# Transposed scores on array tiles and a second softmax built on VectorE, in a fused cross-attention and maxout kernel

## The chip, the cores and the metric

The kernel runs on one core of one Trainium2 chip. The metric is the device time of the whole kernel in microseconds (us), of which several executions are taken. A core has a matrix engine (TensorE, PE in the profile; PEld are its weight loads), VectorE (DVE), ScalarE (ACT), GpSimd (POOL) and SyncE (SP), which here only issues transfers. Each engine works through its own instructions in order and waits for the others by semaphores. Matrix products land in a memory called PSUM, of which the kernels use eight banks; VectorE or ScalarE empties a bank ("evacuates" it) before TensorE uses it again.

## The reference

Per batch b and head h (8 each), x is 512 tokens by 64 and the state is 32 rows (n) by 64. There are two attentions over the same scores, one normalized over the 32 rows, one over the 512 tokens; then a feed-forward layer with a maximum over three products.

```python
scores  = scale * x @ state.T;   a  = softmax(scores,  over n)        # 512 x 32
xread   = a @ state
scores2 = scale * state @ x.T;   a2 = softmax(scores2, over tokens)   # 32 x 512
sread   = a2 @ x
y = concatenate([xread, sread], over tokens), heads side by side      # 8 x 544 rows, 512 wide
h = maximum(y @ w1, y @ w2, y @ w3)                                   # 768 wide
out = h @ w_out
```

The kernels work in bf16 with f32 sums. Both fold the state into the weights: M = state @ w (the "M units") is made per batch, and the product y @ w of the token rows becomes a @ M, so xread is never formed.

## The kernel before

Everything is ordered by hand: a list of short words says what is issued when. `idle n` stands for n filler matmuls on zeros, `lx`, `lw`, `lo` for loads, `pm` for the permutation and cast of x, `xT` for its transposes on TensorE and `xb` for those by a transposing transfer (the "crossbar"), `S` for scores and softmax, `aT` and `ab` for the transposes of a, `R` for the state reads (sread), `M` for M units, `u` for one product a @ M with its evacuation, `o` for half an output tile. In the profile these are known by their PSUM tiles: px (transposes of x), ps (scores), pr (state reads), pa (transposes of a), pm (M units), pw (products a @ M), po (output products), pz (fillers).

```python
OPENING = """
id, idle 9, sel, idle 9, pm 0 0 a, pm 0 1 v, lx 1, xT 0 0 v, lw 2 4, pm 1 1 v, pm 1 0 v,
xT 0 1 a, idle 8, lw 1 2, lw 0 1, S 0 0 g, S 0 1 g, xT 1 1 a, xT 1 0 a, R 0, lw 4 6,
... (cut)
PERIOD = """
u u u P L S S o o u M M m o u u o u u u o u u o X u M m m R u o u u u o u u
"""
# ... cut
def scores(b, h, eng):
    ps = bank([128, 2, 2, HP, Ns], F32, "ps")
    for jj in range(2):
        for hp in range(HP):
            mm(ps[:, jj, :, hp, :], xT(b)[:, 2 * h + jj, hp, :], sbd[:, b, hp, :, :], ...)
    # ... exp on ScalarE to e; reduce over n, reciprocal, product a = e * rden
def state_reads(b):
    # ... cut: pd = ones.T @ e gives the sums over tokens, 8 matmuls in 128x64 mode
    for hp in range(HP):
        for j in range(J):
            mm(psr[:, hp, :, :], x_nat(b)[:, j, 2 * hp:2 * hp + 2, :], e[:, j, :, hp, :], ...)
    # ... cut: AT = psr * reciprocal(pd)
def up(g, m, i):
    pw = bank([128, S], F32, "pw")
    for par in range(2):
        mm(pw, M_sb[:, g, m, par, i, :], aT(g)[:, :, par, :], par == 0, par == 1)
    # i = 0: ScalarE copies pw to t;  i = 1, 2: VectorE takes the maximum of t and pw
```

Tokens lie on the partitions: a softmax over n is then a reduction along the free axis, but a needs a transpose before it can multiply M.

The softmax here doesn't subtract the row's maximum and nothing guards it: scores larger than these inputs give would overflow.

## Time and profile before

| | before |
|---|---|
| time, median (range) | 159.68 us (159.11 to 159.83, 4 runs) |
| span of the profiled run | 157.9 us |
| busy PE / DVE / ACT / POOL | 150.1 / 111.9 / 94.7 / 44.4 us |
| first product pw starts | 18.01 us |
| start of reads in the middle | every 15.66 us |
| last matmul ends (modelled) | 154.4 us, 3.5 us ahead of the end |

TensorE is at 95%, and the chain that ended last is TensorE's for the most part. (This chain is the work followed back from the last instruction, at each step to what released it.) The page's chain part gives the shares of the span by engine:

```profile
PE 79%; DMA 10%; POOL 4%; ACT 3%; issue 1%; DVE 1%; SPq 0%; POOLq 0%
```

What is not TensorE's in it lies in the first 31 us and in the tail.

### The profile page before, as it was taken

The numbers are of one execution on the slowest core, as the hardware profiler recorded it, in microseconds if no ns is written. First come the engines' busy times: TensorE is split into PE (matmuls) and PEld (weight loads), VectorE is DVE, ScalarE is ACT, GpSimd is POOL, SyncE is SP. The second block draws the span as 40 slices with busy tenths as digits, with TensorE's granted clock in tenths as the row PEclk, the third lists the DMA queues.
The fourth block names the chain that finished last, engine by engine and source line by source line (L and its number), as shares of the span: only waits on it lengthen the run. The fifth ranks groups of instructions, "written<-read, shape, count | busy, mean of one in ns | idle before, by whom it ended". The sixth has DMA issues, their size and how long they took to land.

```text
span 157.9 us, 3558 instructions
## 1 busy us (share of the span) xinstructions
PE 150.1 (95%) x1387; PEld 75.4 (48%) x1404; DVE 111.9 (71%) x200; ACT 94.7 (60%) x188; POOL 44.4 (28%) x48
## 2 busy tenths in 40 slices
PE   6988999999999999999999999999999999999991
PEld 2456353354455454444444544454444567754450
DVE  3257999787569788968896888688868844378601
ACT  3559978758545855686567656764777433344340
POOL 8926970292530830091008001300130000000000
PEclk9999999999999999999999999999999999999999
DMA  5999999969549499909990609260316033030263
GB/s 153 291 194 188 182 163 179 204 85 188 162 65 252 106 211 125 254 18 170 160 263 25 184 0 243 59 171 0 137 44 156 4 133 133 0 133 4 66 191 141
DMA packets 34400, 21.46 MB, mean 136 GB/s; under 512 B 19536, under 2 KB 31824, under 8 KB 34384
## 3 DMA queue, kind: packets, MB, share of 16 engines
q0 software_dynamic: 14400, 6.82, 33.9%
q1 hardware_dynamic: 19840, 14.29, 33.4%
q8 instruction: 11, 0.18, 0.4%
q10 hardware_dynamic: 144, 0.13, 0.2%
q14 instruction: 5, 0.04, 0.1%
HBM read 15.20 MB, written 8.91 MB: 153 GB/s over the span
## 4 chain that ended last, share of the span: by engine, by line
PE 79%; DMA 10%; POOL 4%; ACT 3%; issue 1%; DVE 1%; SPq 0%; POOLq 0%
PE pw L106 38%; PE po L106 28%; DMA x<-in_x_dram 10%; PE pm L106 4%; PE pr L106 3%; PE ps L106 2%; POOL a L246 2%; PE px L109 1%; ACT M_sb L101 1%; POOL xn L103 1%; PE pz L106 1%; ACT e L238 1%; ACT xn L101 1%; PE pa L109 1%; POOL x L153 1%
## 5 line engine op out<-in xcount | busy, mean ns | idle before, releaser
L106 PE MATMUL pw<-aT,M_sb 128*128 128x512 bf16 x288 | 71.9, 379 | 0.0
L106 PE MATMUL po<-wout,ht 128*128 128x512 bf16 (+1 forms) x194 | 51.1, 373 | 0.8
L304 DVE TENSOR_TENSOR t<-t,pw 128x512 bf16<-128x512 bf16 (+1 forms) x54 | 35.4, 656 | 19.0 <-PE pw L106 8.9
L300 ACT CAST t<-pw 128x512 bf16<-128x512 f32 (+1 forms) x54 | 30.6, 568 | 29.1 <-PE pw L106 28.8
L106 PEld LDWEIGHTS <-M_sb 128*128 128x128 bf16 x288 | 27.0, 98 | 30.8 <-issue 0.8
L306 DVE TENSOR_TENSOR ht<-t,pw 128x512 bf16<-128x512 bf16 (+1 forms) x54 | 35.2, 657 | 6.8 <-PE pw L106 3.0
L246 POOL TENSOR_TENSOR a<-e,rden 128x512 bf16<-128x512 bf16 x16 | 16.4, 1043 | 59.3 <-ACT e L238 36.3
L101 ACT CAST M_sb<-pm 128x384 bf16<-128x384 f32 x75 | 31.0, 505 | 1.3 <-PE pm L106 0.6
L101 ACT COPY o<-po 128x512 f32<-128x512 f32 x32 | 18.8, 586 | 18.6 <-PE po L106 16.1
L106 PEld LDWEIGHTS <-ht 128*128 128x128 bf16 x210 | 19.7, 98 | 21.3 <-issue 1.9
L103 POOL COPY xn<-x 128x2048 bf16<-128x2048 bf16 x6 | 11.3, 1889 | 8.1 <-DMA x<-in_x_dram 8.1
L106 PE MATMUL pm<-W,sbd 64*32 64x384 bf16 x384 | 12.4, 327 | 0.3 <-DMA W<-in_moe_w_dram 0.2
L242 DVE TENSOR_REDUCE den<-e 128x16 f32<-128x512 bf16 x16 | 10.6, 661 | 2.3 <-ACT e L238 2.2
L238 ACT ACTIVATE e<-ps 128x512 bf16<-128x512 f32 x16 | 9.0, 598 | 4.6 <-PE ps L106 4.6
L103 DVE CAST M_sb<-pm 128x384 bf16<-128x384 f32 x21 | 10.6, 534 | 0.0
L144 POOL DMA_DIRECT2D W<-in_moe_w_dram x12 | 9.1, 772 | 3.4 <-DMA x<-in_x_dram 2.9
L106 PE MATMUL pw<-AT,W 128*128 128x256 bf16 x72 | 9.2, 273 | 0.1
L106 PE MATMUL pz<-zeros 128*128 128x512 bf16 x25 | 7.8, 470 | 1.2 <-DVE zeros L125 1.2
L106 PEld LDWEIGHTS <-sbd 64*32 64x32 bf16 x384 | 4.3, 89 | 9.5 <-issue 8.9
L106 PEld LDWEIGHTS <-W 128*128 128x128 bf16 x72 | 7.0, 98 | 2.5
L279 DVE RECIPROCAL rd<-pr 128x128 f32<-128x128 f32 x8 | 7.6, 944 | 0.1
L153 POOL DMA_DIRECT2D x<-in_x_dram x7 | 6.6, 943 | 0.1
(39 smaller groups left out, 66.9 us busy)
## 6 DMA issues: line engine op xcount, KB each, us to landing
out_dram<-o SPq DMA_DIRECT2D x14, 512.0 KB, 2.9
x<-in_x_dram POOLq DMA_DIRECT2D x7, 512.0 KB, 7.9
W<-in_moe_w_dram POOLq DMA_DIRECT2D x6, 256.0 KB, 7.9
x<-in_x_dram SPq DMA_DIRECT2D x1, 1024.0 KB, 6.6
W<-in_moe_w_dram POOLq DMA_DIRECT2D x6, 128.0 KB, 10.9
wout<-in_moe_w_out_dram POOLq DMA_DIRECT2D x1, 768.0 KB, 12.7
out_dram<-o SPq DMA_DIRECT2D x3, 256.0 KB, 2.1
st<-in_state_dram SPq DMA_DIRECT2D x1, 512.0 KB, 3.7
```

The source lines that it names most:

```text
L101: nc.scalar.copy(out=o, in_=i)
L103: ENG[eng].tensor_copy(out=o, in_=i)
L106: nc.tensor.matmul(out_ap, lhsT, rhs, start=start, stop=stop, tile_position=pos)
L144: nc.gpsimd.dma_start(out=W[:, i, :, c], in_=w_v[i][:, :, c])
L153: nc.gpsimd.dma_start(out=x_sb[b].rearrange("p h j d -> p h (j d)"), in_=x[b].rearrange("h (p j) d -> p h (j d)", j=J))
L238: nc.scalar.activation(out=e.rearrange("p r n -> p (r n)"), in_=ps.rearrange("p j a hp n -> p (j a hp n)"), func=AF.Exp, scale=scale)
L242: nc.vector.reduce_sum(out=den, in_=e, axis=AX.X)
L246: ENG[eng].tensor_mul(out=a_of(b)[:, 2 * h:2 * h + 2].rearrange("p j a hp n -> p (j a hp) n"), in0=e, in1=rden.unsqueeze(2).to_broadcast(( ...
L279: nc.vector.reciprocal(out=rd, in_=pd.rearrange("p (hp n) -> p hp n", hp=HP))
L300: nc.scalar.copy(out=t[:, :nn], in_=pw[:, :nn])
L304: nc.vector.tensor_max(t[:, :nn], t0[:, :nn], pw[:, :nn])
L306: nc.vector.tensor_max(ht[:, m, :nn], tiles["t", g, m][:, :nn], pw[:, :nn])
```

## The change

The intent is to take work off TensorE. The scores are made transposed, rows (head, n) on the partitions and 512 tokens along the free axis, by eight matmuls on eight 64x32 tiles of the array. Then a @ M needs no transposes of a. The softmax over tokens becomes a free-axis matter: the exp gives its row sums as a by-product, and a scalar product scales; its result a2 goes through the crossbar back to token rows for the state reads, which lose their eight matmuls for the sums. The softmax over n now crosses partitions; VectorE does it with a reduce that transposes 32x32 blocks and a 32x32 transpose. Some maxima pass through ScalarE (`w` units). The loads of the opening are re-ordered, and a tiny GpSimd copy ("held") keeps the other loads back until the first half of x has landed. All the order lists are new.

```diff
-id, idle 9, sel, idle 9, pm 0 0 a, pm 0 1 v, lx 1, xT 0 0 v, lw 2 4, pm 1 1 v, pm 1 0 v,
-xT 0 1 a, idle 8, lw 1 2, lw 0 1, S 0 0 g, S 0 1 g, xT 1 1 a, xT 1 0 a, R 0, lw 4 6,
 ... (cut)
+id, lx 1, p0 0 0 v, p0 0 1 v, ca 0 v, p0 1 0 a, ca 1 v, xT 0 0 a, p0 1 1 v, lw 0 1, sel,
+lw 2 4, xT 0 1 v, S 0, pm 1 1 g, pm 1 0 v, lw 4 6, idle 11, D 0 0 g, xT 1 0 a, xT 1 1 v,
+D 0 1 v, M 0 0 aa, lx 2, S 1, D 1 0 g, M 1 0 aa, idle 9, u 0 0 0, M 0 3 aa, D 1 1 g,
+lw 1 2, lx 3, M 0 2 av, M 1 2 aa, u 0 0 1, u 0 0 2, u 0 3 0, u 0 3 1, lo, E 0 g,
 ... (cut)
+u 0 1 2, M 1 4 va, xb 3, S 2, u 0 5 2, u 1 1 1 v, E 2 g, u 1 1 2, R 0 a, u 1 4 0,
+o 0 0 0 a, lx 4, u 1 4 1, o 0 0 1 a, M 2 4 av, M 2 5 av, D 2 0 g, R 1 a, eb 2, o 0 1 0 v,
+o 0 1 1 a, M 2 3 aa, M 2 2 aa, M 2 0 aa, u 1 5 2, o 0 2 0 a, o 0 2 1 a, o 0 3 0 a,
+o 0 3 1 a, D 2 1 v, M 2 1 vv, S 3, u 1 4 2, R 2 v
 PERIOD = """
-u u u P L S S o o u M M m o u u o u u u o u u o X u M m m R u o u u u o u u
+e w u w X w w u o P u w o u u u m m M O B L o w u R M M M d w o u u o u S w O o
 ... (cut)
+    def hold():
+
+        if not held:
+            held.append(const.tile([128, 1], F32, name="held"))
+            nc.gpsimd.tensor_copy(out=held[0], in_=x32[:, 0, 0, 0:1])
 ... (cut)
+    def scores(b):
+        ps = [bank([128, S], F32, "ps") for _ in range(2)]
+        for hp in range(HP):
+            for par in range(2):
+                r = slice(par * 64, par * 64 + 64)
+                mm(ps[par][hp * 32:(hp + 1) * 32, :], sT[r, b, hp, :], xT(b)[r, :, hp, :],
+                   True, True, pos=(par * 64, hp * 32))
+        den2 = tile_of("den2", b, att3, [128, 2], F32)
+        for par in range(2):
+            nc.scalar.activation(out=e_of(b)[:, par, :], in_=ps[par], func=AF.Exp, scale=scale,
+                                 accum_out=den2[:, par:par + 1])
+
+    def softmax_n(b, par, eng):
+
+
+        p = slice(0, 2) if par is None else slice(par, par + 1)
+        k = S // 32 * (2 if par is None else 1)
+        e = e_of(b)[:, p, :].rearrange("p a t -> p (a t)")
+        den = att2.tile([128, 2 * S // 32], F32, tag="den", name="den")[:, 0:k]
+        nc.vector.tensor_reduce(out=den, in_=e.rearrange("p (k n) -> p k n", n=32), axis=AX.X,
+                                op=mybir.AluOpType.add, apply_transpose=True)
+        rden = att2.tile([128, 2 * S // 32], BF16, tag="rden", name="rden")[:, 0:k]
         with nc.allow_low_precision("softmax denom reciprocal"):
             nc.vector.reciprocal(out=rden, in_=den)
-        ENG[eng].tensor_mul(
-            out=a_of(b)[:, 2 * h:2 * h + 2].rearrange("p j a hp n -> p (j a hp) n"),
-            in0=e, in1=rden.unsqueeze(2).to_broadcast((128, 16, Ns)))
-
-    def a_crossbar(b):
+        rb = att2.tile([128, 2 * S], BF16, tag="rb", name="rb")[:, 0:32 * k]
+        nc.vector.transpose(out=rb.rearrange("p (k n) -> p k n", n=32),
+                            in_=rden.unsqueeze(2).to_broadcast((128, k, 32)))
+        ENG[eng].tensor_mul(out=aT(b)[:, p, :].rearrange("p a t -> p (a t)"), in0=e, in1=rb)
+
+    def softmax_t(b, eng):
+        rden2 = att2.tile([128, 2], F32, tag="rden2", name="rden2")
+        nc.vector.reciprocal(out=rden2, in_=tiles["den2", b])
 ... (cut: a2T = e * rden2, one scalar product of 128x512 for each parity)
+    def a2_crossbar(b):
         nc.sync.dma_start_transpose(
+            out=a2(b).rearrange("p a j hp n -> p (a j) (hp n)"),
+            in_=a2T(b).rearrange("p a t -> p (a t)"))
 ... (cut)
+    def state_reads(b, eng):
+        pr = bank([128, HP, 2, Ns], F32, "pr")
         for hp in range(HP):
             for j in range(J):
-                mm(psr[:, hp, :, :], x_nat(b)[:, j, 2 * hp:2 * hp + 2, :], e[:, j, :, hp, :],
+                mm(pr[:, hp, :, :], x_nat(b)[:, j, 2 * hp:2 * hp + 2, :], a2(b)[:, :, j, hp, :],
 ... (cut)
+                nc.scalar.copy(out=t[:, :nn], in_=pw[:, :nn])      # "w" units, i == 1
+                tiles["late", g, m] = eng
 ... (cut)
+            if late:
+                ENG[late].tensor_max(h, h, tiles["t", g, m, 1][:, :nn])
```

In the new lists `S` makes the scores, `D` is the softmax over n, `E` the softmax over tokens, `eb` (in a period `X`) the crossbar transfer of a2; `p0` and `ca` permute and cast batch 0's x and the state in pieces, and `B` is the crossbar's transpose of x. In a period, capital and small letters of a pair (`o` and `O`, `E` and `e`) do the same work with different engines.

## The prediction

> **What bounds the kernel now.** I read the page's busy shares first, then the chain that ended last, then the groups, then the timeline of the opening. The page's head:
>
> ```profile
> span 157.9 us, 3558 instructions
> ...
> PE 150.1 (95%) x1387; PEld 75.4 (48%) x1404; DVE 111.9 (71%) x200; ACT 94.7 (60%) x188; POOL 44.4 (28%) x48
> ...
> PE   6988999999999999999999999999999999999991
> ```
>
> TensorE (PE) is full from the fifth of 40 slices to the last but one. Being busy does not prove it the bound, so I looked at the chain in order of time, in the middle of the run (start us, us, what):
>
> ```profile
> 74.04 0.92 PE pr L106 x24
> ...
> 80.14 0.47 PE ps L106 x16
> ...
> 82.33 0.61 PE pm L106 x24
> ...
> 89.70 0.92 PE pr L106 x24
> ```
>
> Nothing but matmuls lies between. State reads (pr) return after 89.70 - 74.04 = 15.66 us, one period (one batch). Matmuls of 512 columns follow each other in 0.216 us there (ten pw take 2.16 us). A period holds 36 pw (7.78 us) and 24 po (5.18), two groups of M units (pm, 0.61 each), the scores ps (0.47) and the reads pr (0.92): 15.57 us. So the middle is TensorE's instruction stream to within 1%, and only fewer or cheaper matmuls can shorten it.
>
> The opening is bound otherwise. From the timeline:
>
> ```profile
> 1.20 4.02 PE L106 MATMUL pz<-zeros 128*128 128x512 bf16 x9 [1.20 <-DVE zeros L125]
> ...
> 7.85 1.04 ACT L101 CAST xn<-x 128x1024 bf16<-128x1024 f32 x1 [0.62 <-DMA x<-in_x_dram]
> ...
> 11.58 0.63 PE L106 MATMUL ps<-sbd,xT 128*128 128x64 bf16 x16
> ...
> 18.01 1.04 PE L106 MATMUL pw<-aT,M_sb 128*128 128x512 bf16 x4
> ```
>
> Batch 0 lands at 7.85, scores start at 11.6, and the first real product (pw) at 18.0; pz is filler. The last matmul ends near 154.45; copy and store of the last half tile take 3.45 more to 157.9. The timed value is 1.8 us over the span (159.67 against 157.9).
>
> Bookkeeping of useful TensorE work: pw 288 x 0.216 = 62.2; pw of the state rows 72 x 0.108 = 7.8; po 204 x 0.216 = 44; 48 M units x 0.2 = 9.8; ps 8 x 0.47 = 3.8; pr 8 x 0.92 = 7.4; px 6 x 0.45 = 2.7; pa 1.9. Sum 139.5. Some 5.5 of it (scores 0 and 1, four px, one pr, pa of batch 0, five M units) lies before 18.0. After 18.0 there are 134.0 of work in 136.4 us, so all holes together are 2.4 us. Most of them lie in the first overlap of batches 0 and 1, not in the periods.
>
> **What the Trainium skill says.** "TensorEngine Tiling (Array Packing)", Tiling Modes: 64x32 gives 8 independent tiles that run in parallel, and a change of mode drains the engine. The trace agrees: in the chain 24 pm take 0.61 us and 16 take 0.45, so eight matmuls of 384 columns cost 0.16 us, the time of one at full clock, plus about 0.13 for the two changes of mode. "TensorE: Matmul & The Clock Gate", Part 1: matmuls run at half clock until about 3.4 us of activity. The trace agrees: nine pz of 512 columns in 4.02 us at the start (0.43 each), 0.216 later. "VectorE: DVE Perf Modes", the perf-mode tier table: reduce runs at one element a cycle, a two-tensor operation on bf16 in SBUF at two, copies and scalar products at four, with about 150 cycles fixed. The trace agrees with two rows: the reduce of 512 took 661 ns, the bf16 copy xn of 1024 took 423 ns ((256+150)/0.96). The other forms are new here, so their times are estimates from that page.
>
> **The change part by part.**
>
> Scores. Sixteen 64-column matmuls against zero-padded weights become eight of 512 columns on eight tiles: 0.16 x 512/384 + 0.13 = 0.34 us instead of 0.47. Saves 0.13 x 8 = 1.0.
>
> State reads. The eight ones-matmuls for the token denominator go, since exp gives the row sums (accum_out). In the timeline they run from 73.97 to the next group's start at 74.32, and a mode change goes with them: about 0.40. Saves 8 x 0.40 = 3.2.
>
> Array transposes of a (batches 0 to 2): pieces of 0.40, 0.40, 0.55, 0.55. Saves 1.9. The xbar transposes (DMA) move from a to a2, off TensorE.
>
> So TensorE work falls by 6.1 to 133.4, and a period from 15.66 to about 15.1. M units, pw, po and px stay.
>
> VectorE, per period. Goes: two reduces (1.32), their reciprocals (0.50), reciprocal rd (0.94), two scaled AT (0.58), three of the six t maxima (3 x 0.687 = 2.06), one M copy (0.51): 5.9. Comes: transposing reduce over 1024, (1024+150)/0.96 = 1.22; reciprocal of 32, 0.35 (between 253 ns for 16 and 944 for 128); 32x32 transpose 1.22; product of 1024 in bf16 0.69; two scalar products 0.29 each; three late maxima SBUF to SBUF (256+150)/0.96 = 0.42 each; two AT copies 0.58; a tiny reciprocal 0.17: 6.1. It stays at about 13.2 us in 15.1, 88%.
>
> ScalarE, per period: three more copies of pw ("w" units with i = 1), 3 x 0.57 = 1.7, and one more M copy, 0.4. From about 10.3 to 12.5 us of 15.1, 83%. GpSimd loses the products a (two of 1.04) and keeps one permutation of 1.9.
>
> So in the periods TensorE stays the bound, but with two evacuating engines both well over 80%, in order, on eight PSUM banks. I allow 0.1 to 0.3 us of holes a period.
>
> The opening. x of batch 0 comes in two halves with the state between, and GpSimd holds all other loads until the first half is in. From the old landing times (state, 0.5 MB, at 4.4; 1.5 MB by 7.85) I put the halves at 4.4 and 8.0. ScalarE has the second half's cast before the copy of xT's first half, so scores 0 come near 10.2 (11.6 before). But x of batch 1 is now issued at 4.4 instead of 1.44; issue to landing was 5.8 to 9.7 us, so it lands at 10.2 to 13. On VectorE its permutation stands ahead of the first softmax: 0.42, then reduce, reciprocal, transpose for the first parity (0.66 + 0.25 + 0.69), a product on GpSimd (1.04), behind its own permutation and three W issues of 0.77. The second parity ends about as late. aT of batch 0 is whole at 15 to 17, and the order has nine fillers (1.9 us) just before the first pw. I put that pw at 16.5, against 18.0.
>
> Before it fewer useful matmuls have run: two score sets (0.7), px 1.8, two M units 0.4, so 133.4 - 2.9 = 130.5 remain. With the old 2.4 us of holes the end is 16.5 + 130.5 + 2.4 + 3.45 = 152.85 in span, 154.6 timed. The overlap of batches 0 and 1 is tighter, though: from first pw to the third state read TensorE has about 27 us, and my counts give ScalarE 26 (24 M copies at 0.42, 18 t at 0.57, four exps, four o, four AT) and VectorE 26. Three engines equally full do not mesh perfectly; I add 0.7. Predicted: 155.3.
>
> **Rivals.** (1) The first pw does not come earlier. If the late x of batch 1 and a cold clock (no filler runs before the first transposes now; eleven fillers after scores 0 would take 4 us cold instead of 2.4) put it at 18.5, the time is 157.3. For: the long single-file chain above. Against: the fillers are placed as if to bridge a known wait. (2) Evacuation becomes the bound: the softmax over n is a 3.5 us block on VectorE, in which TensorE makes up to eight banks' worth; with 0.5 us of holes in each of seven periods the time is again 157 to 159 and the gain is gone. For: 88% and 83%. Against: VectorE was as full before with holes under 1%, and half of the maxima in question now leave PSUM through ScalarE. (3) Everything meshes and x of batch 1 lands by 10: first pw at 15, holes 2 us: 152.5.
>
> **Range and chances.** The 6.1 us of matmul work is nearly certain; the start (plus or minus 1.7) and the holes (minus 1 to plus 3) are not. That gives 151.8 to 158.6. The 2% line is 156.5, 1.2 us above the middle: faster 0.67, same 0.30, slower 0.03.
>
> **What would show it.** Right: state reads (pr) 15.0 to 15.3 us apart in the chain, still all PE; pr in groups of 16 near 0.5 us; first pw between 15 and 17.5; ScalarE near 109 us busy, VectorE near 113. Wrong: waits of PE or weight loads for DVE or ACT inside the periods (rival 2), a transposing reduce or transpose well over 1.3 us, an exp with row sums well over 0.6 us, an a2 transpose that state reads wait for, or a first pw at 18 or later (rival 1).

## The result, and the profile after

The changed kernel took 164.81 us in the median (164.10 to 166.53, 4 runs), against 159.68 (159.11 to 159.83). The ratio of the fast runs is 1.0344 (95% interval 1.0257 to 1.0432): slower. A ratio here is always the mean time of one kernel's fast runs over that of the other's in the same rounds, so it is not quite the ratio of the medians quoted. The prediction said 155.3 us, with 158.6 as the upper end of its range: wrong in size and in sign.

The page's head of the changed kernel: span, busy times, and TensorE's busy tenths in 40 slices of the span.

```profile
span 162.9 us, 3323 instructions
...
PE 146.7 (90%) x1246; PEld 70.0 (43%) x1246; DVE 115.8 (71%) x211; ACT 106.1 (65%) x232; POOL 43.8 (27%) x44
...
PE   0569899988999978999999999999999999999960
```

TensorE has 3.4 us less busy time, but the span is 5.0 us longer. The slices to look at are the first three (0, 5, 6, where before had 6, 9, 8), the dip to 7 and 8 in slices 15 and 16 (57 to 65 us), and the last two (6, 0). The shares of the chain that ended last say the same:

```profile
PE 68%; DMA 13%; POOL 8%; DVE 6%; ACT 1%; issue 1%; SPq 1%; DVEq 0%; ACTq 0%; POOLq 0%
```

TensorE's share fell from 79% to 68%. GpSimd, VectorE and transfers stand in the chain now.

**The opening.** The timeline of the changed kernel, TensorE's lines and one of VectorE's (start us, us, engine, line, operation, tiles; in brackets idle time ahead and what ended it):

```profile
5.49 1.15 PE L117 MATMUL px<-ident,xn 128*128 128x128 bf16 x8 [5.49 <-POOL held L156]
...
11.06 4.88 PE L114 MATMUL pz<-zeros 128*128 128x512 bf16 x11
15.73 1.22 PE L117 MATMUL px<-ident,xn 128*128 128x128 bf16 x16
16.99 0.69 DVE L111 COPY xT<-px 128x1024 bf16<-128x1024 bf16 x1 [3.22 <-PE px L117]
...
18.24 2.12 PE L114 MATMUL pz<-zeros 128*128 128x512 bf16 x9
...
20.19 0.59 PE L114 MATMUL pw<-aT,M 128*128 128x512 bf16 x2
```

TensorE does nothing until 5.49, so its clock is still low (the trace's clock record has it at full speed only from 16.06 on; before from 5.92): eleven fillers take 4.88 us, 0.44 each, where nine later ones take 2.12. They stand in order ahead of the transposes of batch 1 (px at 15.73), whose input was permuted by 13.01. VectorE's next instruction is the copy of these, and it waits 3.22 us for it with the second half of batch 0's softmax queued behind. So the first pw starts at 20.19 instead of at 18.01 before, though the scores of batch 0 start at 10.50, 1.1 us earlier than before. This run had the clock late: in e2, e3 and e4 below, with the same opening, it came at 13.9 to 14.8 and the first pw at 19.1 to 19.6.

**The middle.** Pieces of the chain in order of time (start us, us, what):

```profile
40.04 3.11 POOL a2T L299 x2
...
43.17 7.15 DMA a<-a2T
...
50.37 0.64 PE pr L114 x16
...
54.22 7.39 DMA a<-a2T
...
61.66 0.64 PE pr L114 x16
...
77.13 0.47 PE pr L114 x16
...
80.90 0.43 PE pw L114 x2
81.33 0.34 PE ps L114 x8
81.67 0.54 PE pw L114 x2
...
92.42 0.47 PE pr L114 x16
```

Up to 61.66 the state reads wait for the crossbar. What TensorE waited for there is one line of the view of its waits (us in total, times, longest):

```profile
PE pr L114 <- DMA a<-a2T: 2.6, 3, 1.6
```

From then on the chain is all TensorE, and a period is 92.42 - 77.13 = 15.29 us (61.2 for four of them), against 15.66 before. The crossbar's time from issue to landing, from the view of the tile a, is:

```profile
DMA to landing us min/median/max: 3.0/4.2/8.5
```

Issue by issue: 7.2 to 8.5 us where GpSimd's loads (the software queue) move 0.5 to 1.0 MB meanwhile, 5.0 us where they move 0.1 MB, and 3.0 to 3.3 us late in the run, beside stores only (in e5 below, 3.7 to 4.5 us there).

**The tail.** Timeline of ScalarE, and of the store queue, changed kernel:

```profile
154.98 0.58 ACT L109 COPY o<-po 128x512 f32<-128x512 f32 x1 [0.71 <-PE po L114]
157.67 0.58 ACT L109 COPY o<-po 128x512 f32<-128x512 f32 x1 [2.10 <-PE po L114]
...
151.28 4.83 SPq L381 DMA_DIRECT2D out_dram<-o  x8
```

The copies of the output tiles run every 1.3 us with 0.71 of idle time between, but the last full one stands 2.10. By the view, its product released it, but another copy's slot in the rotation would have been 156.3: of the two output buffers, the one it needs was presumably still being read by the stores, the eight small ones of the state rows (issued from 151.28 on) among them. In e2, e3, e5, e6 and e13, which also have two buffers, the view of the same copy does name the stores (`<-DMA out_dram<-o`), with 1.07 to 2.43 us of idle time. The end of the span is 5.4 us behind the last matmul, against 3.5 before.

**The new operations.** Groups by form (busy us, mean ns of one):

```profile
L299 POOL TENSOR_SCALAR a2T<-e,rden 128x512 bf16<-128x512 bf16 x6 | 9.7, 1627 | 1.5 <-DVE rden L293 1.5
L281 DVE TRANSPOSE_TENSOR_REDUCE den<-e 128x32 f32<-128x1024 bf16 x5 | 6.2, 1245 | 0.2
...
L271 ACT ACTIVATION_READ_ACCUMULATOR e<-ps 128x1 f32 x16 | 3.2, 201 | 0.0
```

The transposing reduce costs what was estimated, and so does the 32x32 transpose, with the same mean of 1245 ns. The row sums of an exp cost an instruction of their own, 201 ns. The scalar product on GpSimd takes 1.63 us in the mean; the same on VectorE has a median of 351 ns.

**Holes and work.** I took the gap from the start of each matmul to the start of the next, from the first pw to the last matmul, and put it down to the first one's tile. This counts work and waiting together. Of the gaps, those over 0.15 us longer than the matmul itself are called holes; twelve in before of 0.21 to 0.23 us, the length of one matmul whose record is missing from the trace, are left out.

| first pw to last matmul's start | before | after |
|---|---|---|
| pa (array transposes of a) | 0.91 | 0 |
| pr (7 sets, 8 sets) | 5.76 | 4.23 |
| ps (6 sets) | 2.79 | 2.03 |
| pm (43, 46 units) | 9.46 | 9.97 |
| po and pw, with the holes before what follows them | 116.32 | 119.94 |
| sum, with px at 0.9 each | 136.1 | 137.1 |
| of this, holes over 0.15 us | 0.5 | 4.2 to 4.4, by what is taken as a matmul's length |

TensorE is thus 2.7 us better off in the groups that the change touches (0.91 + 1.53 + 0.76 - 0.51), and 3.6 to 3.9 us worse off in holes.

### The profile page after: what moved, and what is told of

Read it like the earlier page. It is cut to its first block, busy times and chain, and to the rows that moved or that the text cites. A ratio compares the mean times of both kernels' runs of the same rounds, so it can differ in the third digit from the quotient of the medians.

```text
span 162.9 us, 3323 instructions
## 1 busy us (share of the span) xinstructions
PE 146.7 (90%) x1246; PEld 70.0 (43%) x1246; DVE 115.8 (71%) x211; ACT 106.1 (65%) x232; POOL 43.8 (27%) x44
## 4 chain that ended last, share of the span: by engine, by line
PE 68%; DMA 13%; POOL 8%; DVE 6%; ACT 1%; issue 1%; SPq 1%; DVEq 0%; ACTq 0%; POOLq 0%
PE pw L114 33%; PE po L114 23%; DMA a<-a2T 9%; POOL a2T L299 4%; DMA x<-in_x_dram 4%; PE pm L114 3%; PE pz L114 3%; PE px L117 2%; PE pr L114 2%; POOL W L162 1%; DVE rb L287 1%; PE ps L114 1%; DVE den L281 1%; DVE xT L111 1%; POOL xn L111 1%
## 5 line engine op out<-in xcount | busy, mean ns | idle before, releaser
L114 PE MATMUL pw<-aT,M 128*128 128x512 bf16 x288 | 71.2, 380 | 0.2 <-DVE M L111 0.2
L331 ACT CAST t<-pw 128x512 bf16<-128x512 f32 (+1 forms) x54 | 30.6, 573 | 19.0 <-PE pw L114 18.7
L114 PEld LDWEIGHTS <-M 128*128 128x128 bf16 x288 | 26.6, 98 | 34.1 <-issue 4.1
L109 ACT CAST M<-pm 128x384 bf16<-128x384 f32 x76 | 31.0, 502 | 3.8 <-PE pm L114 3.5
L111 POOL COPY xn<-x 128x2048 bf16<-128x2048 bf16 (+1 forms) x7 | 12.7, 1808 | 25.9 <-DMA x<-in_x_dram 18.6
L339 DVE TENSOR_TENSOR t<-t,pw 128x512 bf16<-128x512 bf16 (+1 forms) x27 | 17.6, 652 | 2.1 <-PE pw L114 2.0
L336 ACT CAST t<-pw 128x512 bf16<-128x512 f32 (+1 forms) x27 | 15.6, 580 | 2.1 <-PE pw L114 1.8
L345 DVE TENSOR_TENSOR ht<-ht,t 128x512 bf16<-128x512 bf16 (+1 forms) x27 | 12.0, 443 | 2.5
L114 PE MATMUL pm<-W,sT 64*32 64x384 bf16 x384 | 12.1, 327 | 0.0
L287 DVE STREAM_TRANSPOSE rb<-rden 128x512 bf16<-128x512 bf16 (+1 forms) x11 | 10.5, 954 | 0.5
L281 DVE TRANSPOSE_TENSOR_REDUCE den<-e 128x16 f32<-128x512 bf16 (+1 forms) x11 | 10.4, 946 | 0.2
```

Source lines behind the costliest of these rows:

```text
L109: nc.scalar.copy(out=o, in_=i)
L111: ENG[eng].tensor_copy(out=o, in_=i)
L114: nc.tensor.matmul(out_ap, lhsT, rhs, start=start, stop=stop, tile_position=pos)
L281: nc.vector.tensor_reduce(out=den, in_=e.rearrange("p (k n) -> p k n", n=32), axis=AX.X, op=mybir.AluOpType.add, apply_transpose=True)
L287: nc.vector.transpose(out=rb.rearrange("p (k n) -> p k n", n=32), in_=rden.unsqueeze(2).to_broadcast((128, k, 32)))
L331: nc.scalar.copy(out=t[:, :nn], in_=pw[:, :nn])
```

## The experiments

Theories: (A) the opening is slow because of the cold clock; (B) the first state reads (batches 0 to 3) come too early for the crossbar; (C) the tail is held by a third use of two output buffers; (D) GpSimd is too slow for the scalar products; (E) the hold, or the order of the loads, delays what follows. The rival to A and B taken together is that the overlap of batches 0 and 1 is bound by evacuation anyway, so that what is won in one place is lost at the next wait.

In five calls fifteen kernels ran (e1 to e4, e5 to e8, e9 to e12, e13 and e14, e15), all with right results; the kernel before ran in each call (160.53 us in the median in the last, 159.56 to 160.33 in the others). With one core a run is called slow when it is over 1.5% above the fastest of its kernel.

### e1_warm: fillers at the start only

```diff
-id, lx 1, p0 0 0 v, ...
+id, idle 9, lx 1, p0 0 0 v, ...
```

> Edit: nine filler matmuls before anything else on TensorE, as the kernel before has; nothing else. Theory A (a cold clock in the single-file opening): the eleven fillers after scores 0 take 2.4 us instead of the 4.88 of the changed kernel, the transposes of x of batch 1 start near 13.3 instead of 15.7, the first pw comes near 17.2 to 17.8 instead of 20.2, and the time falls by 2 to 3 us, to about 162. Rival B (the state reads' wait for the crossbar of a2 sets the end, and the chain on GpSimd and DMA before it does not start earlier): the first pw comes earlier, but the time falls by less than 1 us and the holes before the state reads grow.

Measured: 168.63, 171.75, 164.90, 171.68 us, three of them slow, so there is no ratio to rely on; the one fast run equals the changed kernel. The clock row of the profiled run, which is one of the slow ones (tenths of full speed in 40 slices), says why:

```profile
PEclk9957999999999995999999999999999999999998
```

(The row shows 9 also ahead of the first grant.) The fillers warmed the clock from 4.6 us on, but the thin stretch of short transposes behind them lost it again from 8.0 to 14.8, and the first pw came at 19.58. A second dip stands at 62.6 to 66.0 us, behind a hole of 2.77 us that ended with a state read. Fillers at one place are not a warm clock; A is neither confirmed nor refuted by this run.

### e2_softmax_t_on_dve: the scalar products of batches 0 to 2 on VectorE

```diff
-... lo, E 0 g,  ... E 1 g, eb 1, ...  E 2 g, ...
+... lo, E 0 v,  ... E 1 v, eb 1, ...  E 2 v, ...
```

> Edit: the token softmax (a2T) of batches 0 to 2 on VectorE instead of GpSimd. Rival B: GpSimd is late and takes 1.6 us for each product against 0.35 on VectorE, so the crossbars of a2 start 3 to 5 us earlier and the TensorE holes before state reads 0 and 2 (0.87 and 0.50 us) go; the hole before state read 3 (1.77) stays, as its product is on VectorE already. Time lower by 1 to 1.5 us. Theory A: first pw stays at 20.2 and the time changes by under 0.7 us, since the holes come back elsewhere (VectorE is full there).

Measured: 164.48 and 164.66 (fast), 167.99 and 172.77 (slow); ratio of fast runs 1.0301 (1.0252 to 1.0351) against 1.0344 for the change, within the noise of both. The holes before the state reads moved (1.2 before that of batch 2, 1.6 before that of batch 4) and did not go. D alone is not the cause.

### e3_late_reads: the state reads of batches 0, 2 and 3 later

```diff
-... E 2 g, u 1 1 2, R 0 a, u 1 4 0,
-... D 2 0 g, R 1 a, eb 2, o 0 1 0 v,
-o 0 3 1 a, D 2 1 v, M 2 1 vv, S 3, u 1 4 2, R 2 v
+... E 2 g, u 1 1 2, u 1 4 0,
+... D 2 0 g, R 0 a, R 1 a, eb 2, o 0 1 0 v,
+o 0 3 1 a, D 2 1 v, M 2 1 vv, S 3, u 1 4 2
+FIRST = """e w u w X w w u Q o ... S w O R o"""    # first period; Q is the read of batch 2, R the next
```

> Edit: state reads 0, 2 and 3 stand later in TensorE's order (0 beside 1, 2 inside the first period, 3 at that period's end); everything else as in the changed kernel. If the waits for the crossbar of a2 cost what the trace shows, the three holes of 0.87, 0.50 and 1.77 us go and the time falls by 2.5 to 3 us; if TensorE is held by something else there (evacuation, banks), the holes move and the time falls by under 1 us.

Measured: 163.98 to 165.74, ratio 1.0320 (1.0262 to 1.0378): no gain. The waits of the reads shrank from 2.6 to 0.4 us as wanted, but TensorE then waited elsewhere:

```profile
PE ps L117 <- DMA xT<-xn: 1.7, 1, 1.7
```

The scores of batch 4 are then too early for the crossbar's transposes of x. Removing one wait alone uncovered the next one, as the rival has it.

### e4_third_o: three output buffers instead of two

```diff
-    op = ctx.enter_context(tc.tile_pool(name="op", bufs=2))
+    op = ctx.enter_context(tc.tile_pool(name="op", bufs=3))
```

> Edit: three output buffers instead of two. In the changed kernel the last full copy of an output tile stood 2.1 us idle until 157.67 with its matmuls done near 156.3, and the end came 5.3 us after the last matmul against 3.45 before. If it waits for the buffer that the eight state-row stores still read, a third one lets it go at 156.3 and takes 1.0 to 1.5 us off the end. If the end is set by the stores' own queue, nothing changes (under 0.4 us).

Measured: 163.89 and 164.42 (fast), 166.89 and 168.46 (slow); ratio 1.0275 (1.0222 to 1.0327). The last full copy now keeps the rhythm of the others (it starts at 155.59, 1.30 us after the one ahead, with 0.71 us of idle time):

```profile
155.59 0.58 ACT L109 COPY o<-po 128x512 f32<-128x512 f32 x1 [0.71 <-PE po L114]
```

The wait for a buffer is confirmed: the same copy idles 0.71 us in e4, e7 and e14, with three buffers, and 1.07 to 2.43 us in the changed kernel, e2, e3, e5, e6 and e13, with two. Its worth is less sure. From the end of the last matmul to the end of the span it is 161.6 - 156.9 = 4.7 us instead of 5.4, 0.65 us, and not the 1.0 to 1.5 expected; but this compares single profiles, and with two buffers this stretch is 4.4 us in e5 and 5.7 in e3. The remaining 1.3 us over before's tail lie behind the last issue: the last half tile's store is issued at 157.35 and the span ends 4.2 us later, against 3.0 us before (154.92 to 157.9). About half of it, 0.6 us, comes after the stores: from the landing of the last one to the end of the span, where only drains and semaphore instructions stand, it is 1.66 us in e4 and 1.05 before. As to the other 0.7: the eight small stores are issued 6.8 us ahead of the last, where before had 9.4 us; whether they are the reason was not tested.

### e5_filled: fillers in all gaps of the opening

```diff
-id, lx 1, ... xT 0 0 a, p0 1 1 v, lw 0 1, sel,
-lw 2 4, xT 0 1 v, S 0, ...
+id, idle 9, lx 1, ... xT 0 0 a, idle 4, p0 1 1 v, lw 0 1, sel,
+lw 2 4, idle 3, xT 0 1 v, idle 5, S 0, ...
```

> Edit: the changed kernel with fillers in every gap of TensorE before scores 0 (9 at the start, 4, 3 and 5 between the transposes). The first experiment failed to keep the clock: it was granted at 4.6 us, taken away again from 8.0 to 14.8. Theory A: with the gaps filled the clock stays at full from about 5 us on, the eleven fillers take 2.4 us, the first pw comes at 17 to 17.8 instead of 20.2. The time falls by 2 to 3 us if the opening is what sets the end; rival C (loads): the loads behind the first pw are issued by GpSimd in order behind the softmax, so they start only 2 us earlier and the state reads wait more: time falls by under 1 us.

Measured: 165.91, 166.12, 167.96 (fast), 168.95 (slow); ratio 1.0452 (1.0384 to 1.0520), slower still. Yet the opening did what A expects: the first pw starts at 17.3 instead of 20.2. The clock row and the pieces of the chain, in order of time, of the same profiled run (a fast one):

```profile
PEclk9999999999996999999999999999999999999999
...
40.36 8.99 DMA a<-a2T
...
49.40 0.64 PE pr L114 x16
```

TensorE gets to the reads earlier, but the a2 of batches 2 and 4 (landed at 49.4 and 78.5, against 50.3 and 73.4) are no earlier by as much, or later: the holes in front of these reads are 2.83 and 2.82 us now, and behind the first of them the clock is at half speed for 3.41 us (50.2 to 53.6). A gain of 2.9 us at the front was more than lost behind.

### e6_loads_first: no hold, all loads issued early

```diff
-D 0 1 v, M 0 0 aa, lx 2, S 1, ...  lw 1 2, lx 3, ...  lo, E 0 g,
+D 0 1 v, M 0 0 aa, lx 2, lw 1 2, lx 3, lo, S 1, ...  E 0 g,
-        if not held:
+        if False:
```

> Edit: the hold on the first loads is taken off, and the last weights, x of batch 3 and the output weights are issued by GpSimd before the softmax products of batch 1 instead of behind them. Rival C: the software DMA queue no longer runs dry at 24 to 26 us, its opening loads end near 33 instead of 37.5, the crossbars of a2 0 and 1 land 3 us earlier, and the holes before state reads 0 and 2 (0.87, 0.50) go; time falls by 1 to 3 us. Theory A: first pw stays near 19.5 to 20.2 and the time changes by less than 1 us.

Measured: 166.91 to 169.21, ratio 1.0517 (1.0440 to 1.0595). By the timeline the cast of the second half of batch 0's x starts at 10.13, where it starts at 8.01 in the changed kernel. The hold is thus worth 2.1 us to that half; scores 0 slip from 10.5 to 12.6 and the first pw to 22.6. The first half of E is refuted: the hold helps. The order of the loads by itself is tried in e12.

### e7_all_undone: fillers, late reads, third buffer, VectorE products and e6's loads together

> Edit: fillers in the gaps, no hold and the loads first, token softmax of batches 0 to 2 on VectorE, third output buffer, late state reads. If the causes named (cold opening, late loads and crossbars, the output buffer) are the whole excess, then the work saved on TensorE shows: 156 to 159 us, under the kernel before. If it stays above 161, a cause is still missing.

Measured: 159.98 to 161.02, ratio 1.0067 (1.0035 to 1.0100). The suspects together carry nearly all of the loss, though 160.5 us in the median is not the 156 to 159 that was expected if they were all of it. One new hole shows a collision, in the timeline of all engines:

```profile
24.55 2.31 DVE L302 TENSOR_SCALAR a2T<-e,rden 128x512 bf16<-128x512 bf16 x2
24.56 1.89 POOL L114 COPY xn<-x 128x2048 bf16<-128x2048 bf16 x1 [1.14 <-DMA x<-in_x_dram]
...
27.51 0.36 PE L117 MATMUL pm<-W,sT 64*32 64x384 bf16 x8 [2.12 <-DVE ht L346]
```

Two scalar products of 0.35 us took 2.31 us on VectorE, because a GpSimd copy of 1.89 us started 0.01 us after the first of them, and TensorE stood 2.12 us for it. The Trainium skill, "SBUF — State Buffer", section "Who interferes with whom", says that VectorE's fast modes and GpSimd share one pair of ports under an exclusive lock, and that the one that does not have it stands for the whole instruction. The trace agrees: the pair of products ends at 26.86, 0.41 us after the copy's end at 26.45, about the time of one product.

### e8_before_cold: the kernel before without its first 18 fillers

```diff
-id, idle 9, sel, idle 9, pm 0 0 a, pm 0 1 v, lx 1, ...
+id, sel, pm 0 0 a, pm 0 1 v, lx 1, ...
```

> Edit: the kernel before without its 18 fillers ahead of the first transposes (the 8 before scores 0 stay). Theory A: its clock is granted only near 12 to 16 us too, the first pw comes 1 to 3 us later than 18.0 and the time rises by 1 to 3 us. If the opening's clock does not matter (rival B or C): under 0.7 us.

Measured: 161.16 to 163.40, ratio 1.0190 (1.0132 to 1.0248), 3 us. Two lines of its timeline:

```profile
10.71 3.07 PE L106 MATMUL pz<-zeros 128*128 128x512 bf16 x8
...
19.98 1.04 PE L106 MATMUL pw<-aT,M_sb 128*128 128x512 bf16 x4
```

Eight fillers take 3.07 us instead of 1.89, and the first pw comes 2.0 us late. This is theory A by itself, in a kernel without any other part of the change: the 18 fillers that the change left out are worth 3 us to the kernel before.

### e9_mended to e12_mended_late_loads: the mended kernel with one part put back at a time

e9 is e7 with the hold put back and batch 0's scalar products earlier (`D 1 1 g, E 0 v`). e10 takes the early fillers out of e9, e11 puts the state reads of batches 0, 2 and 3 back to where the change has them, e12 puts the loads back to where the change has them.

```diff
 e9 (on e7):  -if False:   +if not held:        -... u 0 3 1, E 0 v,   +... D 1 1 g, E 0 v,
 e10:  -id, idle 9, lx 1, ... idle 4, ... idle 3, xT 0 1 v, idle 5, S 0   +id, lx 1, ... xT 0 1 v, S 0
 e11:  -... R 0 a, R 1 a, eb 2 ... (FIRST with Q)                       +... R 0 a, u 1 4 0, ... R 1 a, eb 2, ... R 2 v
 e12:  -lx 2, lw 1 2, lx 3, lo, S 1, ...                                +lx 2, S 1, ... lw 1 2, lx 3, ... lo
```

> Edit: the changed kernel with every mend but the hold kept: fillers in the gaps, later loads issued before the softmax products, token softmax of batches 0 to 2 on VectorE and that of batch 0 moved ahead of GpSimd's permutation (in the last set it met that copy and took 2.31 us instead of 0.6, with a TensorE hole of 2.4), late state reads, third output buffer. First pw at 17 to 17.5, no hole over 1 us after it, full clock from 5 us on. If these are the causes: 157 to 159 us, below the kernel before (159.6). If over 160.5, something is still missing.

> Edit: as e9_mended without the fillers. Against e9 this gives the cost of the cold clock when nothing behind it waits: theory A says 2 to 3.5 us more than e9 (the kernel before lost 3.1 us in the same test); rival C says under 1 us.

> Edit: as e9_mended with the state reads where the changed kernel has them. If waits for the crossbar of a2 cost time by themselves: holes of 1 to 3 us before state reads 2 and 3, perhaps with 3.4 us of half clock[...], and 2 to 5 us more than e9. If they only fill a time that is lost anyway: within 0.7 us of e9.

> Edit: as e9_mended with the last weights, x of batch 3 and the output weights issued where the changed kernel has them, behind the softmax products. If the loads' place costs time by delaying crossbars and x: 1 to 2 us more than e9. If late reads and fillers are enough: within 0.7 us of e9.

Measured:

| | us (fast runs) | ratio to before |
|---|---|---|
| e9 | 160.17 to 160.85 | 1.0012 (0.9955 to 1.0069) |
| e10, no early fillers | 161.59 to 163.92 | 1.0144 (1.0053 to 1.0236) |
| e11, early reads | 161.48, 163.55; slow 167.28, 167.52 | 1.0137 (1.0026 to 1.0248) |
| e12, late loads | 159.75 to 160.22 | 0.9983 (0.9929 to 1.0037) |

e9 has the fillers of the opening at full clock, and e10 has its first pw late again:

```profile
10.71 2.55 PE L117 MATMUL pz<-zeros 128*128 128x512 bf16 x11
...
17.39 0.59 PE L117 MATMUL pw<-aT,M 128*128 128x512 bf16 x2
```

```profile
20.01 0.59 PE L117 MATMUL pw<-aT,M 128*128 128x512 bf16 x2
```

Without the fillers the first pw falls back from 17.39 to 20.01, and the medians differ by 1.75 us. In e9 itself one expectation failed, that no hole over 1 us is left: at 21 us TensorE waits 1.9 us for a copy of M on VectorE, which stands behind batch 0's scalar products; these take 1.14 and 1.28 us instead of 0.35.

The early reads cost 2.0 us in the mean of the two fast runs (161.48 and 163.55, at a mean granted clock of 1.0), and scatter the times. No fast run of e11 was profiled, so why they cost this is not seen. The profiled run is a slow one, and its clock row has two dips, behind holes of 3.07 and 2.78 us:

```profile
PEclk9999996999999999999599999999999999999999
```

Neither hole stands before a read that was moved: the first ends at 24.3 us, ahead of any read, in code that e9 has too, and the second stands before the read of batch 4. The moved reads waited 0.05 us at most in it.

The order of the loads is worth nothing. So putting back one thing costs about 2 us for A, with the trace to show why, and about 2 us for B, for which the reason has to come from e13.

### e13_two_mends: the changed kernel with e5's fillers and e3's late reads, nothing else

> Edit: the changed kernel with only two mends, the fillers in the gaps and the late state reads (token softmax on GpSimd, loads, hold and two output buffers as in the change). If these two are the causes: 160.5 to 161.5 us, that is the best so far (160.1) plus the 0.7 to 1.3 us of the output buffer. If the token softmax on GpSimd matters by itself: 162 or more.

Measured: 160.25, 160.92, 161.28 (fast), 164.17 (slow); ratio 1.0051 (0.9984 to 1.0118). Alone, the late reads brought 0.2% and the fillers lost 1.1%; together they bring 2.9% of the 3.4%. The two are not a sum: an earlier opening only makes the reads wait longer, and later reads only help once TensorE gets there earlier. The waits of the state reads in e5 and in e13, both profiled in fast runs and different in the place of the reads alone:

```profile
PE pr L114 <- DMA a<-a2T: 5.6, 3, 2.7
```

```profile
PE pr L117 <- DMA a<-a2T: 1.2, 1, 1.2
```

These 4.4 us and e5's 3.41 us at half clock (some 1.7 us lost), less 1.2 us that the scores now wait for the crossbar of x, account for the 5.0 us between the two profiled spans (163.6 and 158.6). So B is shown here: with the opening mended, it is the reads' wait for the crossbar that costs. Against e3 the fillers gain 4.1 us in the mean; of the 3.3 us between the two profiled spans, 2.3 lie ahead of the first pw and 1.1 in the tail.

### e14_token_softmax_moved, e15_weights_in_time: is there a gain in the rest?

```diff
 e14 on e13:  -u 0 3 1, lo, E 0 g,  ... E 1 g, ... E 2 g    bufs=2
              +u 0 0 2, E 0 v, u 0 3 0, ... E 1 v, ... E 2 v    bufs=3
 e15 on e14:  -lx 2, S 1, ... u 0 0 0, M 0 3 aa, D 1 1 g,   lw 1 2, lx 3, M 0 2 av, ...
              +lx 2, lw 1 2, S 1, ... u 0 0 0, u 0 0 1, u 0 0 2, D 1 1 g,   lx 3, M 0 3 aa, M 0 2 av, ...
```

> Edit: as e12_mended_late_loads, with the token softmax of batch 0 a few units later, where GpSimd does not read SBUF. In e12 it took 1.51 us for 0.7 of work and a TensorE hole of 1.09 us followed. If the shared port explains it: hole gone, 159.0 to 159.5 us, below the kernel before. If VectorE is simply full there: the hole moves, 159.8 to 160.3.

> Edit: as e14_token_softmax_moved, with the last weights issued right behind x of batch 2, and the M units that waited for weights moved behind the first three products. In e14 TensorE stood 1.0 us twice for weights still on their way (at 19.0 and 30.3). If these two holes are the rest: 158 to 159 us in the fast state, 0.5 to 1% below the kernel before, which would be the first version to beat it. If VectorE and ScalarE are full there anyway: 159.3 to 160.

Measured: e14 159.58, 159.78, 159.88 (fast), 165.47 (slow), ratio 0.9989 (0.9911 to 1.0067). e15 159.05 to 160.82 (four fast of six), ratio 0.9951 (0.9896 to 1.0005), in five rounds. In e14 no collision is left: all sixteen products take 346 to 354 ns, where the longest in the changed kernel took 1918. What TensorE still waited for in e14, and in e15 after the weights were loaded in time:

```profile
PE pm L117 <- DMA W<-in_moe_w_dram: 1.9, 2, 1.0
```

```profile
PE ps L117 <- DMA xT<-xn: 1.1, 1, 1.1
PE pw L117 <- DVE M L114: 0.8, 1, 0.8
```

The waits for weights fell from 1.9 to 0.5 us, and waits of 1.9 us came in other places. No version clearly beats the kernel before; the best only draws level.

## Why the prediction was wrong, step by step

In the profiled run, timed 165.22 us, the error is 9.9 us: first pw 3.7 late, 3.8 more from there to the end of the last matmul (137.4 instead of the 130.5 + 3.1 that the prediction put), 1.9 more in the tail, 0.5 more between span and time.

**The opening: "I put that pw at 16.5, against 18.0". This is the first step that failed.** It took over the times of TensorE's pieces at full clock. The prediction named the cold clock as rival 1 with the right mechanism ("eleven fillers after scores 0 would take 4 us cold instead of 2.4"; they took 4.88), and then set it aside because "the fillers are placed as if to bridge a known wait". They bridge the wait until 13.01 and then stand 2.7 us in the way of px, for which VectorE waits. e9 against e10 (first pw 17.39 against 20.01, 1.75 us in time) and e8 (3 us in the kernel before) show what the cold clock costs. With a warm clock the opening falls only 0.9 us short of the prediction. No run takes the eleven fillers out, so whether that would do as well as warming them is open.

**The holes: "With the old 2.4 us of holes", plus 0.7. This is the second.** The step took the crossbar transfer of a2 as "off TensorE" and gave it no time. For batches 0 to 2 it takes 3.1 to 3.4 us of products on GpSimd, and 7.2 to 8.5 us in transfer where loads of 0.5 MB and more run beside it, and three state reads stood 2.6 us for it. "An a2 transpose that state reads wait for" was on the list of what would show the prediction wrong, but in no sum. e5 against e13 shows what these early reads cost once TensorE gets to them in time; e3 and e5 show that neither this nor the opening can be mended alone. Measured by gaps, holes rose by 3.6 to 3.9 us from before to after, where I had 0.7. The old "2.4 us of holes" was itself no such thing: holes of over 0.15 us in before come to 0.5, and the rest of the 2.4 is small change between matmuls, which the bookkeeping had too low.

**The work saved: "TensorE work falls by 6.1".** The mechanism was right and the size was not. pr in groups of 16 came out at 0.47 us (0.52 was implied) and ps at 0.34, exactly as put. But the term "plus about 0.13 for the two changes of mode" covers only one of the two. The change back is paid by the matmuls that follow. In the chain of the changed kernel, shown above, two pw take 0.43 at 80.90 and 0.54 at 81.67, behind the scores. Before, the scores ran in the same mode as what followed, and nothing was added there:

```profile
80.14 0.47 PE ps L106 x16
80.60 1.29 PE po L106 x6
```

Six po at 0.216 are 1.29. So the scores save 0.47 - 0.34 - 0.11 = 0.02 us and not 0.13. For the reads it is likewise: before, M units stood right ahead of the pr, whose 0.92 us held the change out of their mode; now M units follow the pr, and the next two pw pay it (0.54). The reads save 0.92 - 0.47 - 0.11 = 0.34 and not 0.40. Both together are 0.36 a batch, which is what the periods show (15.66 - 15.30), instead of 0.53. Over eight batches the 6.1 us become 6.1 - 8 x 0.17 = 4.7 (worked out).

**VectorE and ScalarE: right.** 115.8 us of busy time against "near 113", 106.1 against "near 109". Reduce and transpose of 1024 took 1245 ns against 1.22; the late maxima in SBUF have a median of 425 ns against 0.42; the scalar product of VectorE 351 against 290. The product of 1024 in bf16 has a median of 0.692 against 0.69; its mean is 0.93 because one of the five took 1.86 us, beside a GpSimd copy (80.6 to 82.5). Missed were such collisions and the 201 ns behind each exp (3.2 us in all, ScalarE had room). In the periods from 61.66 on, no holes stand in the chain: rival 2 in the form "evacuation becomes the bound in each of seven periods" did not happen.

**The tail: "copy and store of the last half tile take 3.45 more".** It was carried over from before, while the last part of the schedule had been rewritten. e4 shows the wait for a buffer, worth some 0.65 of the 1.9 us in its profile; 0.6 more lie behind the landing of the last store.

**What happened to the gain.** Even mended, the change draws level and does not win. For e14 (157.6 us of span) against before (157.9) the stretches are: first pw 0.5 us earlier, the stretch to the end of the last matmul 0.5 shorter (135.9 against 136.4), the tail 0.7 longer. The saving of 4.7 us went, first, into the opening: before 18.01 us the old kernel had done 5.5 us of useful matmuls, the new one does some 2.9 (both from the prediction's bookkeeping), so 2.6 us more remain to be done, with a start only 0.5 us earlier. Second, holes in the overlap of batches 0 and 1 are 2.2 us in e14 against 0.5. Third, the tail. That is 2.1 + 1.6 + 0.7 = 4.4 us, and with the 0.3 us by which the span is shorter, the whole 4.7; a gap of 0.42 us at 36.0 between M units and scores is not counted, so the sum is good to about that. The first overlap is where the prediction feared "three engines equally full"; e15, where part of the wait for weights turned into one for VectorE (0.8 us) with little change in time, fits that, but its longest wait, for the crossbar's transpose of x, stands at 77 us, in a period, and what each remaining hole costs was not separated and stays open. Open also is whether the eight small stores lengthen the tail.

Two sums of the prediction do not come out of their own terms, and neither matters for the result: rival 3 gives 152.75 and not 152.5, and the errors named for the start and the holes reach from 152.6 to 160.0 about 155.3, not from 151.8 to 158.6. The 150 cycles that it takes from the page "VectorE: DVE Perf Modes" are stated there in other sections than the table it names.

The scatter of the changed kernel's times (164.1 to 166.5, and up to 172.8 in e2) against 1.0 to 2.1 us from lowest to highest of before's seven runs in a call may be the clock in part: e5's and e6's profiles, both fast runs, have 3.41 us of half clock behind a hole before a state read. It is not the clock alone: e13's slow run (164.17) and its fastest (160.25) have the same mean granted clock, 0.995. In the changed kernel's own profiled run the longest hole was 1.77 us and the clock stayed up. No run tests the scatter itself.

## What to carry to other kernels

Work taken off the busiest engine pays only where that engine is fed; before counting it, walk through the opening, the first overlap and the tail and ask what each new wait hangs on and how late that comes. When a mechanism turns up in the prediction as a rival (here the cold clock and the crossbar's latency), give it its measured number in the sum rather than argue it away. Mends of two waits in a row must be tried together: each alone can look worthless or harmful.

## What the Trainium skill lacked or had wrong

- "TensorEngine Tiling (Array Packing)", Key Properties, says that a change of tiling mode drains the engine, but gives no cost. Here it was about 0.11 us on the matmuls behind each change (two pw 0.54 against 0.43 us, six po 1.40 against 1.29), as much as half a 512-column matmul, paid on leaving the mode as well as on entering it.
- "TensorE: Matmul & The Clock Gate", "HAM oscillation — how this bites in real kernels", warns of idle gaps over about 3.4 us. Holes of 2.64 us (e6) and 2.83 us (e5) in fast runs were already followed by 3.41 us at half clock, while a second hole of 2.82 us in e5 and those of up to 2.4 us were not (the free-running window that the page's Part 1 describes would fit that; no run tests it).
- "DMA: Bandwidth & Descriptors", "Queues, rings and completion order", says that a completion lands only after earlier writes of the same DMA engine, across queues; it has no number for what this does to a crossbar transpose. Here it took 3.0 to 3.3 us beside stores only (3.7 to 4.5 us in e5) and 7.2 to 8.5 us beside software-queue loads of 0.5 to 1.0 MB. Whether completion order or shared bandwidth does it, no run here tells apart.
- "GPSIMD Engine Reference", "4.1 Engine selection", calls one-input operations on GpSimd roughly line-rate. A scalar product of 128x512 in bf16 took 1.58 us there (median), against 0.35 us on VectorE, while a copy of four times as many elements (128x2048) took 1.89 us: by these numbers the words fit the copy and not the scalar product.
- No page has the cost of an exp's accumulator output: each was followed by an instruction of 201 ns on ScalarE.
